# Five scheduling edits in a memory-recurrent attention and gated MLP training kernel: row blocks of the first projections, the queues of lead-in loads, and where two bulk copies stand

## The chip, the cores and the metric

The kernel runs on one core of one Trainium2 chip, as one launch. The metric is the device time of that launch in microseconds (us), taken as the median of several executions. The engines are TensorE (PE, with its weight loads shown apart as PEld), VectorE (DVE), ScalarE (ACT), GpSimd (POOL) and SyncE (SP); SP, ACT and POOL also issue DMA transfers.

## The reference, cut to what matters

The program computes a forward pass and all its gradients. S = 2048 tokens of width D = 640, H = 32 heads of width 128, segments of 32 tokens, M = 8 memory rows, hidden width F = 1728.

```python
xn = layernorm(x)
mem = mem0
for s in range(64):                       # segments, one after the other
    h = concat([mem, xn[:, 32*s:32*s+32]])            # 40 rows
    q, k, v = h @ Wq, h @ Wk, h @ Wv
    p = softmax(where(mask, q @ k.T / sqrt(128), -1e9))
    o = (p @ v) @ Wo
    mem = o[:8]; outs.append(o[8:])
g = silu((silu(xn @ w1) * (xn @ w3)) @ w2)
out = x + concat(outs) * g
# outputs: out, and the gradients of x, mem0, Wq, Wk, Wv, Wo, w1, w3, w2 under grad_out
```

Since each segment's memory rows come from the segment before, the attention part is a chain of 64 steps forward, and of 64 steps backward.

## The kernel before, in words

The kernel is a sequence of stages that share one core. Inside most stages the instructions of each engine keep the order in which they are written (`in_order` ties every instruction to the one before it on its engine), so a wait on one engine holds up all that is written behind it on that engine, and a DMA issue that waits holds up the later issues on its queue.

1. **`phase12_ln_Bfwd`** (0 to 283 us): layer norm and forward MLP. At its end, while the last MLP tiles (`up`) are interleaved, it computes V for the first `NB0` = 672 tokens in full 512-column products, and stores it to the DRAM tensor `QVX`.
2. **`first_part`** (283 to 406 us): the same first 672 rows for K (`KX`) and then Q (`QVX`). Each of these three projections goes through `first_rows` (L356): for a block of 112 rows (6 blocks) and a group `cg` of 1024 columns (4 groups), two PSUM tiles of 112 x 512, each with five accumulating matmuls (640 = 5 x 128), an eviction by DVE or ACT into a staging tile, and a store. During the K projection the stage also loads `Wq` and `Wo` (`fetch`), turns `Wv` head by head on PE and stores it to `WVT` (`turn_w`), and later turns the first K rows (`kload`, `kturn`). The loop index `n` counts row block and column group together, 0 to 47; loads and clears are tied to values of `n`.
3. **`recurrence`** (406 to about 1640 us): 64 forward steps. Each step projects the 32 x 640 activations of its segment in a packed form (`packed_half`): four matmuls of 32 rows each stand side by side in the PE array, at column positions 0, 32, 64 and 96, each with another group of 1024 weight columns.
4. **`phase3b_out`** (to about 1794 us): the rest of the output projection, and the turned weights `WoT`, `WqT`, `WkT` by transposing DMA loads. It also builds the list `later`: 16 DRAM-to-DRAM copies that the backward chain issues one per step on the POOL queue, from step t = 53 on. The first two are the copies of the token rows of the gradient `GS` into `GWO`, which holds token and memory rows in blocks of 120.
5. **`phase4_Abwd`** (1794 to 2995 us): a lead-in of 19 units `pro` (a unit is a tile of three segments and four heads), and then 64 backward steps. A unit is loaded by `ld`, turned on PE with ACT evictions into `gvT` and `gOT` (`turn`), multiplied (`dprob`), put through the softmax gradient on DVE (`dsoft`) and reduced to memory rows (`gmem`). `ld` issues four loads: memory rows `QVM`, token rows `QVS` (both into `gqv`), the gradient `gor`, and the probabilities `PR` (into `gPr`). For the first 19 units three of the four are issued on POOL and the fourth on SP; later units use SP for all. The stores of `gvT` to `VTD` and of `gdS` to `DSR` are issued on POOL, each out of two buffers.
6. **`phase6_Awgrads`** (2995 to 4224 us): gradients of Wv, Wk, Wq and of the attention input. Eight rounds `qd` of 512 columns; a round has 22 positions `p` (one unit each) and then the weight gradient itself, 15 long sums `wg` at L1562. `ld_w` (L1444) loads three weight slices per round: Wv from its stored turned copy `WVT`, Wk and Wq by transposing DMA loads (`turned_load`, L271). `ld` (L1456) loads a unit ahead, five units at most. In the first round `ld_to(3)`, `ld_w(0)` and `ld_to(5)` stand in this order on the SP queue.
7. **`phase6b_gWo`** and **`phase5_Bbwd_ln`** (4224 us to the end): the gradient of Wo, which reads `GWO`, and the backward MLP and layer norm.

Of the kernel before, what the change touches and what calls it, by code (L numbers as in the profile page):

```python
# [9 lines left out]
BF16 = mybir.dt.bfloat16  # L10
F32 = mybir.dt.float32
# [5 lines left out]
P = 128  # L17
# [23 lines left out]
class K:  # L41
# [109 lines left out]
    def setup_dram(self):  # L151
        tc = self.tc
        S, D, T, H, F = self.S, self.D, self.T, self.H, self.F
        HD = self.HD
        dp = self.ctx.enter_context(tc.tile_pool(name="scratch", bufs=1, space=bass.MemoryType.DRAM))
        self.dp = dp
        mk = lambda name, shape, dt=BF16: dp.tile(list(shape), dt, name=name, uniquify=False)
        self.XN = mk("XN", (S, D))
        self.SLT = mk("SLT", (F, S))
        self.DUT = mk("DUT", (F, S))  # L160
        self.HB = mk("HB", (F, S))
        self.DZ = mk("DZ", (S, D))
# [36 lines left out]
        self.GSP = mk("GSP", (8, 3, 160, 512))  # L199
        self.WVT = mk("WVT", (P, H, D))  # L200

    def x_src(self, tl, w, c0, c1):
        return self.tok_src(96 * tl, self.geo(tl)[2], w, c0, c1)
# [65 lines left out]
def turned_load(k, dst, src):  # L269

    k.nc.sync.dma_start_transpose(dst, src)  # L271
# [83 lines left out]
    return pt  # L355


def first_rows(k, ps, stage, xs, off, W, dst, x0, cg, nb=112, tag="b0pb", w=1024, q=None):

    nc = k.nc  # L360
    for b in range(2):
        c0 = cg * 1024 + b * 512
        if w == 512 or b == 0:
            st = stage()
        pb = ps.tile([nb, 512], F32, name="b0pb", tag=tag)
        for dc in range(k.DC):
            nc.tensor.matmul(pb[:], xs[:, dc, x0 - off:x0 - off + nb], W[:, dc, c0:c0 + 512],
                             start=(dc == 0), stop=(dc == k.DC - 1))
        s0 = b * 512 if w == 1024 else 0
        k.copy(st[:, s0:s0 + 512], pb[:], eng='vs'[b])  # L370
        if w == 512 or b == 1:
            (q or nc.sync).dma_start(dst[x0:x0 + nb, cg * 1024 + (b * 512 if w == 512 else 0):cg * 1024 + b * 512 + 512], st[:])


def phase3_Afwd(k, W4, Wv, Wk_):
# [18 lines left out]
def first_part(k, Wv, Wk_, Wq, Wo, kTs, vt, hxs, rest):  # L394
    nc, tc = k.nc, k.tc
    DC, H, HD = k.DC, k.H, k.HD
    with tc.tile_pool(name="b0", bufs=1) as io, tc.tile_pool(name="b0s", bufs=4) as stp, \
# [4 lines left out]
        xs = io.tile([P, DC, k.NB0], BF16, name="b0x")  # L402
# [45 lines left out]
            turn_w()  # L448
        n = 0
        for W, dst in ((Wk_, k.KX[:, :]), (Wq, k.QVX[:, 0])):  # L450
            for x0 in range(0, k.NB0, 112):
                for cg in range(4):
                    if n % 2 == 1 and fetch:
                        nc.scalar.dma_start(*fetch.pop(0))
                    first_rows(k, ps, lambda: stp.tile([112, 1024], BF16, name="b0st", tag="b0st"), xs, 0, W, dst, x0, cg, q=nc.gpsimd)
                    turn_w()
                    if zero:
                        nc.gpsimd.memset(zero.pop(0)[:], 0.0)
                    if n >= 26 and n % 2 == 0 and (n - 26) // 2 < 9:
                        i = (n - 26) // 2  # L460
                        if i > 0:
                            kturn(i - 1)
                        if i < 8:
                            kload(i)
                    if n == 20:
# [4 lines left out]
                    if n == 44:  # L470
# [435 lines left out]
def phase3b_out(k, Wo, W0, W4):  # L906


    nc, tc = k.nc, k.tc
    D, DC, H, HD, T = k.D, k.DC, k.H, k.HD, k.T  # L910
    WT = {}
# [7 lines left out]
    with tc.tile_pool(name="oio", bufs=1) as io, tc.tile_pool(name="oac", bufs=1, space=bass.MemoryType.PSUM) as pa, \  # L919
# [5 lines left out]
        st, acc = {}, {}  # L925
# [90 lines left out]
        while g0:  # L1016
# [2 lines left out]
        in_order(k, start)  # L1019
    WT["v"] = W4.tile([P, H, D], BF16, name="WvT", tag="w3")  # L1020

    n = k.NTL - 1
    later = [(k.GWO[0:120 * n, :].rearrange("(t r) d -> t r d", r=120)[:, 0:96], k.GS[0:96 * n, :].rearrange("(t r) d -> t r d", r=96)),
             (k.GWO[120 * n:120 * n + 32, :], k.GS[96 * n:k.S, :])]

    for s in range(3):
        t0 = (2, 0, 1)[s]
# [14 lines left out]
def phase4_Abwd(k, out2, WoT, WvT, WkT, WqT, later):  # L1042
# [3 lines left out]
    with tc.tile_pool(name="gst", bufs=1) as st, tc.tile_pool(name="gchain", bufs=1) as ch, \  # L1046
# [185 lines left out]
        def ld(tl, qd, eng=None):  # L1232

            ns, nm, nx, n = k.geo(tl)
            c0, h0 = qd * 512, qd * 4
            i = cnt["l"]
            cnt["l"] += 1
            early = i < len(pro)
            g = i % 6 if early else (i - len(pro) + 1) % NG
            if g < NG:  # L1240
                gor = gors[g][:]
                qv = fl.tile([120, 2, 512], BF16, name="gqv", tag="gqv", bufs=4)[:]
                Pr = fl.tile([120, 4, P], BF16, name="gPr", tag="gPr", bufs=4)[:]
            else:
                x = xb[:, g - NG]
                qv = x[:, 0:1024].rearrange("p (i c) -> p i c", i=2)
                gor = x[:, 1024:1536]
                Pr = x[:, 1536:2048].rearrange("p (h c) -> p h c", h=4)
            t0 = 3 * tl
            q = nc.gpsimd if early else nc.sync  # L1250
            q.dma_start(
                qv[nx:n], k.QVM[t0:t0 + ns, :, qd // 2, :, 512 * (qd % 2):512 * (qd % 2) + 512].rearrange("t r i c -> (t r) i c"))
            k.load_x(qv, 0, k.x_src(tl, "qv", c0, c0 + 512), q)
            k.load_x(gor, 0, k.g_src(tl, c0, c0 + 512), nc.sync)
            q.dma_start(Pr[0:n], k.PR[tl][:, h0:h0 + 4, :])
            uu["l", tl, qd] = qv, gor, Pr

        def turn(tl, qd):
# [152 lines left out]
def phase6_Awgrads(k, X, out0, out3, out4, out5):  # L1411
# [12 lines left out]
    with tc.tile_pool(name="h6i", bufs=3) as io, tc.tile_pool(name="h6", bufs=1) as hp, \  # L1424
# [20 lines left out]
        def ld_w(qd):  # L1445
            c0 = qd * 512
            ws = []
            for i, src in enumerate((k.A_Wv, k.A_Wk, k.A_Wq)):
                w = gp.tile([P, 4, D], BF16, name="w6", tag=f"w6{i}")
                if i == 0:  # L1450
                    nc.sync.dma_start(w[:], k.WVT[:, 4 * qd:4 * qd + 4, :])
                else:
                    turned_load(k, w[:], src.rearrange("d h e -> d (h e)")[:, c0:c0 + 512])
                ws.append(w)
            Ws[qd] = ws
# [145 lines left out]
        for qd in range(8):  # L1601
            u0 = NTL * qd
            for p in range(NTL):
# [113 lines left out]
def phase12_ln_Bfwd(k: K, Wv, Wk_):  # L1717
# [6 lines left out]
    with tc.tile_pool(name="bw", bufs=1) as wp, tc.tile_pool(name="bio", bufs=2) as io, \  # L1724
# [165 lines left out]
        turned_load(k, xb[:, :, 0:224], k.XN[448:672, :])  # L1890
        up_ld(NBLK - 1, 0)
        up_ld(NBLK - 1, 1)
        xa, off = xnTs[NBLK], 0
        stg = []

        def stage():
            stg.append(ln.tile([112, 512], BF16, name="b0st", tag=f"xt{len(stg) % 8}"))
            return stg[-1]
        for n, (x0, cg) in enumerate([(x0, cg) for x0 in range(0, k.NB0, 112) for cg in range(4)]):
            if n % 3 == 1 and n // 3 < TB:  # L1900
                up(NBLK - 1, n // 3)
                if n < 6:
                    up_ld(NBLK - 1, n // 3 + 2)
            if x0 == 448:
                xa, off = xb, 448
            first_rows(k, ps, stage, xa, off, Wv, k.QVX[:, 1], x0, cg, tag="pg", w=512)
        in_order(k, start)


# [271 lines left out]
```

## Time and profile before

| | |
|---|---|
| time, median of 3 | 4798.12 us (4796.45 to 4808.65) |
| span of the profiled execution | 4795.1 us |
| PE busy | 4474.0 us (93%) |
| DVE, ACT, POOL busy | 2248.3, 1591.1, 2109.1 us |
| mean granted TensorE clock | 0.974 of full speed |
| DMA moved | 841.31 MB, mean 175 GB/s |

PE busy over the whole span is the mean over stages with different limits, so the table alone doesn't say what any one edit is worth. The windows view gives, for each stretch of time, the busy time of each engine, the granted clock (PEclk, where 1.00 is full speed) and the mean busy share of the 16 DMA engines; the timeline gives instructions in order, with the idle time before each in brackets and what ended it. In both, a queue's DMA issues are listed as SPq, ACTq or POOL.

### The profile page before, as it was taken

Reading aid. Unit: us, or ns where it says so; the run is one execution under the profiler, and the core shown is the slowest. Engines: PE = TensorE matmul, PEld = TensorE weight load, DVE = VectorE, ACT = ScalarE, POOL = GpSimd, SP = SyncE. Lnnn points to the kernel's source line nnn. Section 1 sums busy time; section 2 is a strip of 40 time slices with the busy share of each in tenths; the row PEclk is TensorE's granted clock in tenths of the full one; section 3 lists DMA queues with packets and bytes.
Section 4 is the critical chain, followed back from the end, with each engine's and each line's share of the span. In section 5 each row is a group of like instructions: output and inputs, shape, how many; then the busy total and the mean of one; then the engine's idle time right before and its main releaser. Section 6 shows DMA issues by size and latency. Waiting matters only on the chain. (4 is left out here: it accounts for less than half of the span.)

```text
span 4795.1 us, 160346 instructions
## 1 busy us (share of the span) xinstructions
PE 4474.0 (93%) x64434; PEld 2864.5 (60%) x64704; DVE 2248.3 (47%) x7164; ACT 1591.1 (33%) x4371; POOL 2109.1 (44%) x3541
## 2 busy tenths in 40 slices
PE   8898999999999787989999998899999999999999
PEld 4455555555555464656666665666666666667665
DVE  8634666666666524545555553332234322311460
ACT  5432555555544522323333332322233222300000
POOL 6522555555555405445544443643355433411340
PEclk9999999999999796999999999899999999999999
DMA  8763566666555497777777773943455433669774
GB/s 271 234 231 101 174 178 180 179 181 181 178 166 169 128 218 206 209 210 207 219 210 208 212 211 111 207 131 108 108 151 154 133 109 106 190 193 223 158 179 98
DMA packets 997844, 841.31 MB, mean 175 GB/s; under 512 B 542558, under 2 KB 880402, under 8 KB 995096
## 3 DMA queue, kind: packets, MB, share of 16 engines
q1 hardware_dynamic: 784201, 552.53, 41.9%
q0 software_dynamic: 130592, 229.98, 16.4%
q10 hardware_dynamic: 82307, 48.52, 3.9%
q8 instruction: 511, 8.37, 0.8%
q14 instruction: 233, 1.91, 0.1%
HBM read 473.80 MB, written 311.48 MB: 164 GB/s over the span
## 5 line engine op out<-in xcount | busy, mean ns | idle before, releaser
L1562 PE MATMUL wg<-gr,hr 128*128 128x512 bf16 x2352 | 519.1, 379 | 2.5
L1543 PE MATMUL g<-w,ghacc 128*128 128x320 bf16 x3072 | 459.8, 300 | 0.8
L1562 PEld LDWEIGHTS <-hr 128*128 128x128 bf16 x2400 | 233.9, 98 | 278.8
L1543 PEld LDWEIGHTS <-ghacc 128*128 128x128 bf16 x3072 | 288.4, 98 | 104.2 <-ACT ghacc L92 2.2
L307 PEld LDWEIGHTS <-hx 128*32 128x32 bf16 x7680 | 176.7, 96 | 168.9 <-issue 5.7
L90 DVE CAST wgo<-wg 128x512 bf16<-128x512 f32 x72 | 49.8, 692 | 471.3 <-PE wg L1562 462.9
L90 DVE CAST stg<-bank 128x512 bf16<-128x512 f32 x256 | 177.0, 692 | 161.4 <-PE bank L307 154.9
L778 POOL DMA_DIRECT2D OR<-xv x163 | 90.4, 555 | 354.0 <-ACT xv L92 334.0
L92 ACT COPY ghacc<-t6g 128x768 bf16<-128x768 bf16 (+1 forms) x176 | 137.2, 780 | 304.1 <-PE t6g L1525 303.1
L1508 POOL DMA_DIRECT2D GSP<-grs x48 | 25.7, 547 | 477.6 <-ACT grs L1500 474.8
L326 PEld LDWEIGHTS <-gkv 128*8 128x8 bf16 x8192 | 179.0, 87 | 89.0 <-issue 7.1
L1268 POOL DMA_DIRECT2D VTD<-gvT x176 | 129.4, 741 | 219.7 <-ACT gvT L1267 199.9
L730 POOL TENSOR_TENSOR xP<-xP,xrz 120x480 bf16<-120x480 bf16 x163 | 161.4, 990 | 75.1 <-DVE xrz L729 46.2
L710 ACT ACTIVATE xP<-xsp,xnm 120x120 bf16<-120x120 f32 (+1 forms) x540 | 186.6, 373 | 20.5 <-DVE xnm L692 17.2
L1549 DVE TENSOR_TENSOR ghacc<-ghacc,g 128x320 f32<-128x320 f32 x192 | 93.5, 487 | 210.0 <-PE g L1543 210.0
L92 ACT CAST wgo<-wg 128x512 bf16<-128x512 f32 x48 | 28.1, 586 | 479.8 <-PE wg L1562 421.4
L1297 DVE SCALAR_TENSOR_TENSOR gdS<-gdp,Dx,gPr 120x120 bf16<-120x120 f32 (+1 forms) x680 | 182.8, 331 | 0.0
L326 PE MATMUL bank<-Wo,oTm 128*32 128x320 bf16 x4032 | 158.2, 312 | 18.8 <-DVE oTm L608 18.8
L326 PE MATMUL gbank<-WvT,gkv 128*8 128x320 bf16 x4096 | 171.0, 311 | 4.6 <-issue 3.6
L1315 POOL DMA_DIRECT2D GXP<-gks x157 | 91.1, 581 | 190.9 <-ACT gks L1313 184.3
L326 PE MATMUL gbank<-WkT,gkv 128*8 128x320 bf16 x4096 | 163.9, 301 | 3.9 <-issue 2.1
L307 PE MATMUL bank<-Wq,hx 128*32 128x512 bf16 x2560 | 163.0, 384 | 2.6 <-DVE stg L90 2.6
(354 smaller groups left out, 10920.6 us busy)
## 6 DMA issues: line engine op xcount, KB each, us to landing
QVS<-stg SPq DMA_DIRECT2D x128, 256.0 KB
vTt<-VTD SPq DMA_DIRECT2D x64, 320.0 KB
VTD<-gvT POOLq DMA_DIRECT2D x168, 120.0 KB, 3.8
DSR<-gdS POOLq DMA_DIRECT2D x168, 120.0 KB, 3.2
dS<-DSR SPq DMA_DIRECT2D x168, 120.0 KB
P<-PR SPq DMA_DIRECT2D x168, 120.0 KB
PR<-xP POOLq DMA_DIRECT2D x163, 120.0 KB, 3.3
OR<-xv POOLq DMA_DIRECT2D x163, 120.0 KB, 3.1
```

The source lines that it names most:

```text
L90: return nc.vector.tensor_copy(out, in_)
L92: return nc.scalar.copy(out, in_)
L307: k.nc.tensor.matmul(bank[32 * g:32 * g + 32, :], x[:, dc, :], W[:, dc, c0:c0 + 512], start=(dc == 0), stop=(dc == k.DC - 1), tile_positio ...
L326: k.nc.tensor.matmul(pm[p0:p0 + nq, 0:320], x[:, h, :], W[:, h, 320 * b:320 * b + 320], start=(first and i == 0), stop=(last and i == 15), ...
L710: nc.scalar.activation(Pb[0:n, j, 0:n], sp[0:n, j, :], ACT.Exp, bias=nmx[0:n, j:j + 1], scale=k.scale, accum_out=Z[0:n, j:j + 1])
L730: eng.tensor_tensor(Pb[0:n, :, 0:n], Pb[0:n, :, 0:n], bc_last(rz[0:n], n), ALU.mult)
L1268: nc.gpsimd.dma_start(k.VTD[tl][:, :, h0:h0 + 4, :], vTq[:])
L1297: nc.vector.scalar_tensor_tensor(dS[0:n, j, 0:n], dp[0:n, j, :], Dx[0:n, j:j + 1], Pr[0:n, j, 0:n], op0=ALU.subtract, op1=ALU.mult)
L1315: (nc.sync if (tl, qd) in pro else nc.gpsimd).dma_start(k.GXP[tl, :, qd, 0:ns], ks[:].rearrange("p s i h m -> p s i (h m)"))
L1543: nc.tensor.matmul(pg[:], ring[:, i, j, r0:r0 + P], Ws[qd][i][:, j, 320 * h:320 * h + 320], start=(i == 0 and j == 0), stop=(i == 2 and j ...
L1549: nc.vector.tensor_tensor(a, a, pg[:], ALU.add)
L1562: nc.tensor.matmul(pw[:], hr[:, tl, dc * P:(dc + 1) * P], grs[i][:, tl, :], start=(tl == 0), stop=(tl == NF - 1))
```

## The change

Five edits:

1. The three first projections use blocks of 128 rows: five blocks of 128, and a rest of 32 rows that is computed by the new `last_rows` in the packed form of the recurrence. `n` then runs from 0 to 41, and what was tied to values of `n` is moved. From `n` = 36 on the stores are issued on SP instead of POOL.
2. The V projection at the end of `phase12_ln_Bfwd` puts its two PSUM tiles under two tags (`pg`, `pu`) instead of one.
3. In the lead-in of the backward chain, the loads of `QVS` and `PR` are issued on SP.
4. The slices of `WkT` and `WqT` that the first round of `phase6_Awgrads` needs are stored to a DRAM tensor `WQK` during the backward chain (they take the place of the two `GWO` copies at the head of `later`), and loaded from there with plain DMAs.
5. The copy of the `GS` rows into `GWO` is made in seven pieces and a rest in the rounds of `phase6_Awgrads`, at position p = 18, on POOL.

The purpose is less PE time for the first rows, a shorter queue of loads ahead of the stores in the lead-in, no bulk copy beside the backward chain, and no transposing DMA ahead of the first units' loads.

```diff
-def first_rows(k, ps, stage, xs, off, W, dst, x0, cg, nb=112, tag="b0pb", w=1024, q=None):
+def first_rows(k, ps, stage, xs, off, W, dst, x0, cg, tag="b0pb", w=1024, q=None):
...
-        pb = ps.tile([nb, 512], F32, name="b0pb", tag=tag)
+        pb = ps.tile([P, 512], F32, name="b0pb", tag=tag if isinstance(tag, str) else tag[b])
         for dc in range(k.DC):
-            nc.tensor.matmul(pb[:], xs[:, dc, x0 - off:x0 - off + nb], W[:, dc, c0:c0 + 512],
+            nc.tensor.matmul(pb[:], xs[:, dc, x0 - off:x0 - off + P], W[:, dc, c0:c0 + 512],
...
+def last_rows(k, ps, stage, xs, off, W, dst, tag="b0pb", w=1024, q=None):
+
+    x0 = k.NB0 - 32
+    for b in range(2):
...
+        packed_half(k, pb, xs[:, :, x0 - off:x0 - off + 32], W, b)
+        s0 = b * 512 if w == 1024 else 0
+        k.copy(st[:, s0:s0 + 512], pb[:], eng='vs'[b])
...
@@ first_part
-            for x0 in range(0, k.NB0, 112):
-                for cg in range(4):
+            for x0 in list(range(0, k.NB0 - 32, P)) + [None]:
+                for cg in range(4 if x0 is not None else 1):
...
+                    if x0 is None:
+                        last_rows(k, ps, stage, xs, 0, W, dst, q=nc.gpsimd if n < 36 else nc.sync)
+                    else:
+                        first_rows(k, ps, stage, xs, 0, W, dst, x0, cg, q=nc.gpsimd if n < 36 else nc.sync)
...
-                    if n >= 26 and n % 2 == 0 and (n - 26) // 2 < 9:
-                        i = (n - 26) // 2
+                    if n >= 24 and n % 2 == 0 and (n - 24) // 2 < 9:
+                        i = (n - 24) // 2
...
@@ phase3b_out
-    n = k.NTL - 1
-    later = [(k.GWO[0:120 * n, :].rearrange("(t r) d -> t r d", r=120)[:, 0:96], k.GS[0:96 * n, :].rearrange("(t r) d -> t r d", r=96)),
-             (k.GWO[120 * n:120 * n + 32, :], k.GS[96 * n:k.S, :])]
+    later = [(k.WQK[i], WT[w][:, 0:4, :]) for i, w in enumerate("kq")]
...
@@ phase4_Abwd, ld
             q = nc.gpsimd if early else nc.sync
...
-            k.load_x(qv, 0, k.x_src(tl, "qv", c0, c0 + 512), q)
+            k.load_x(qv, 0, k.x_src(tl, "qv", c0, c0 + 512), nc.sync)
             k.load_x(gor, 0, k.g_src(tl, c0, c0 + 512), nc.sync)
-            q.dma_start(Pr[0:n], k.PR[tl][:, h0:h0 + 4, :])
+            nc.sync.dma_start(Pr[0:n], k.PR[tl][:, h0:h0 + 4, :])
...
@@ phase6_Awgrads, ld_w
-                if i == 0:
-                    nc.sync.dma_start(w[:], k.WVT[:, 4 * qd:4 * qd + 4, :])
+                if i == 0 or qd == 0:
+                    nc.sync.dma_start(w[:], k.WVT[:, 4 * qd:4 * qd + 4, :] if i == 0 else k.WQK[i - 1])
...
@@ phase6_Awgrads, the positions p of a round
+                if p == 18:
+                    if qd < 7:
+                        nc.gpsimd.dma_start(k.GWO[360 * qd:360 * qd + 360, :].rearrange("(t r) d -> t r d", r=120)[:, 0:96],
+                                            k.GS[288 * qd:288 * qd + 288, :].rearrange("(t r) d -> t r d", r=96))
+                    if qd == 6:
+                        nc.gpsimd.dma_start(k.GWO[120 * NTL - 120:120 * NTL - 88, :], k.GS[96 * NTL - 96:S, :])
...
@@ end of phase12_ln_Bfwd
-        for n, (x0, cg) in enumerate([(x0, cg) for x0 in range(0, k.NB0, 112) for cg in range(4)]):
+        for n, (x0, cg) in enumerate([(x0, cg) for x0 in range(0, k.NB0 - 32, P) for cg in range(4)]):
...
-            first_rows(k, ps, stage, xa, off, Wv, k.QVX[:, 1], x0, cg, tag="pg", w=512)
+            first_rows(k, ps, stage, xa, off, Wv, k.QVX[:, 1], x0, cg, tag=("pg", "pu"), w=512)
+        last_rows(k, ps, stage, xb, BLK, Wv, k.QVX[:, 1], tag=("pg", "pu"), w=512)
```

More of the change, by code (lines that the diff above doesn't have):

```diff
@@ L200, in setup_dram @@
         self.WVT = mk("WVT", (P, H, D))
+        self.WQK = mk("WQK", (2, P, 4, D))
     def x_src(self, tl, w, c0, c1):
@@ L371, in first_rows @@
         if w == 512 or b == 1:
-            (q or nc.sync).dma_start(dst[x0:x0 + nb, cg * 1024 + (b * 512 if w == 512 else 0):cg * 1024 + b * 512 + 512], st[:])
+            (q or nc.sync).dma_start(dst[x0:x0 + P, cg * 1024 + (b * 512 if w == 512 else 0):cg * 1024 + b * 512 + 512], st[:])
+def last_rows(k, ps, stage, xs, off, W, dst, tag="b0pb", w=1024, q=None):
+    x0 = k.NB0 - 32
+    for b in range(2):
+        if w == 512 or b == 0:
+            st = stage()
+        pb = ps.tile([P, 512], F32, name="b0pb", tag=tag if isinstance(tag, str) else tag[b])
+        packed_half(k, pb, xs[:, :, x0 - off:x0 - off + 32], W, b)
+        s0 = b * 512 if w == 1024 else 0
+        k.copy(st[:, s0:s0 + 512], pb[:], eng='vs'[b])
+        if w == 512 or b == 1:
+            c0, c1 = (b * 512 if w == 512 else 0), b * 512 + 512
+            (q or k.nc.sync).dma_start(dst[x0:k.NB0].rearrange("r (g c) -> g r c", g=4)[:, :, c0:c1], st[:])
 def phase3_Afwd(k, W4, Wv, Wk_):
@@ L450, in first_part @@
         for W, dst in ((Wk_, k.KX[:, :]), (Wq, k.QVX[:, 0])):
-            for x0 in range(0, k.NB0, 112):
-                for cg in range(4):
+            for x0 in list(range(0, k.NB0 - 32, P)) + [None]:
+                for cg in range(4 if x0 is not None else 1):
                     if n % 2 == 1 and fetch:
                         nc.scalar.dma_start(*fetch.pop(0))
-                    first_rows(k, ps, lambda: stp.tile([112, 1024], BF16, name="b0st", tag="b0st"), xs, 0, W, dst, x0, cg, q=nc.gpsimd)
+                    stage = lambda: stp.tile([P, 1024], BF16, name="b0st", tag="b0st")
+                    if x0 is None:
+                        last_rows(k, ps, stage, xs, 0, W, dst, q=nc.gpsimd if n < 36 else nc.sync)
+                    else:
+                        first_rows(k, ps, stage, xs, 0, W, dst, x0, cg, q=nc.gpsimd if n < 36 else nc.sync)
                     turn_w()
@@ L464, in first_part @@
                             kload(i)
-                    if n == 20:
+                    if n == 18:
                         mem_ld()
@@ L469, in first_part @@
                         nc.gpsimd.memset(kTs[1][:], 0.0)
-                    if n == 44:
+                    if n == 38:
                         for i in range(2):
@@ L1889, in phase12_ln_Bfwd @@
         xb = io.tile([P, DC, BLK], BF16, name="xnT_b", tag="xnT_b")
-        turned_load(k, xb[:, :, 0:224], k.XN[448:672, :])
+        turned_load(k, xb[:, :, 0:160], k.XN[512:672, :])
         up_ld(NBLK - 1, 0)
@@ L1896, in stage @@
         def stage():
-            stg.append(ln.tile([112, 512], BF16, name="b0st", tag=f"xt{len(stg) % 8}"))
+            stg.append(ln.tile([P, 512], BF16, name="b0st", tag=f"xt{len(stg) % 8}"))
             return stg[-1]
-        for n, (x0, cg) in enumerate([(x0, cg) for x0 in range(0, k.NB0, 112) for cg in range(4)]):
+        for n, (x0, cg) in enumerate([(x0, cg) for x0 in range(0, k.NB0 - 32, P) for cg in range(4)]):
             if n % 3 == 1 and n // 3 < TB:
@@ L1903, in phase12_ln_Bfwd @@
                     up_ld(NBLK - 1, n // 3 + 2)
-            if x0 == 448:
-                xa, off = xb, 448
-            first_rows(k, ps, stage, xa, off, Wv, k.QVX[:, 1], x0, cg, tag="pg", w=512)
+            if x0 == BLK:
+                xa, off = xb, BLK
+            first_rows(k, ps, stage, xa, off, Wv, k.QVX[:, 1], x0, cg, tag=("pg", "pu"), w=512)
+        last_rows(k, ps, stage, xb, BLK, Wv, k.QVX[:, 1], tag=("pg", "pu"), w=512)
         in_order(k, start)
```

## The prediction

> **What bounds the kernel now.** I read the windows view first, cut at the stages that the five edits touch, to see which stretches are bound by PE and which wait. Columns: the window, its length, busy us of PE, PEld, DVE, ACT, POOL (with counts), granted PE clock, busy share of the 16 DMA engines, GB/s.
>
> ```profile
> 208.00:283.00 75.00, 69.46 (x357) 42.32 (x356) 29.55 (x49) 20.26 (x34) 13.40 (x20) 1.00 0.48 149
> 289.00:352.00 63.00, 59.40 (x362) 37.37 (x363) 21.77 (x36) 20.78 (x36) 27.63 (x41) 1.00 0.94 331
> 352.00:406.00 54.00, 54.00 (x290) 32.83 (x292) 20.40 (x34) 14.57 (x26) 16.05 (x26) 1.00 0.45 139
> 1794.00:1886.00 92.00, 59.47 (x551) 33.37 (x561) 40.35 (x249) 26.23 (x104) 56.61 (x98) 0.63 0.81 224
> 2082.00:2107.00 25.00, 16.92 (x308) 9.22 (x297) 6.80 (x35) 2.40 (x9) 6.24 (x13) 0.73 0.53 184
> 2996.00:3020.00 24.00, 9.18 (x84) 6.91 (x84) 4.21 (x10) 5.29 (x9) 18.39 (x34) 0.50 1.00 211
> 3107.00:3172.00 65.00, 64.68 (x312) 30.05 (x316) 7.07 (x12) 4.60 (x8) 6.60 (x12) 1.00 0.26 67
> ```
>
> The reader sees three kinds. The V, K and Q projections (first three rows) are PE-bound: 54.00 of 54.00 us in the Q part. The lead-in (1794 to 1886) and the start of the weight-gradient stage (2996 to 3020) have an idle PE at a low clock beside nearly full DMA engines. The window at 2082 lies in the backward chain, with PE at 17 of 25 us, yet the DMA engines half free. The last row, the `wg` sums of a round, has the DMA engines at 0.26.
>
> Then the waits in these stretches. In the lead-in (who waited for what: total, times, longest):
>
> ```profile
> ACT gvT L1266 <- DMA VTD<-gvT: 39.4, 11, 9.1
> DVE gdS L1294 <- DMA DSR<-gdS: 15.5, 6, 5.1
> PE gvpt L1264 <- DMA gor<-GX: 10.0, 1, 10.0
> ```
>
> ACT waits for its two `gvT` buffers, that is for stores that POOL issues behind the loads. Next the timeline. The first two lines are POOL's around step t = 53; the next are SP's and PE's at the start of the weight-gradient stage; the last is one whole packed projection of a backward step.
>
> ```profile
> 2078.62 0.66 POOL L1406 DMA_DIRECT2D GWO<-GS  x1
> 2099.41 0.60 POOL L1315 DMA_DIRECT2D GXP<-gks  x1 [5.73 <-DMA GWO<-GS]
> ...
> 3001.92 5.56 SPq L271 DMA_TRANSPOSE w<-in_A_Wk_dram  x1
> 3007.53 5.91 SPq L271 DMA_TRANSPOSE w<-in_A_Wq_dram  x1
> 3013.48 0.60 SPq L1462 DMA_DIRECT2D dS<-DSR  x1
> ...
> 3016.57 0.58 PE L1483 MATMUL t<-ident,dS 120*128 120x120 bf16 x4 [11.48 <-DMA dS<-DSR]
> ...
> 2975.60 2.34 PE L307 MATMUL gbank<-WoT,gox 128*32 128x512 bf16 x40 [0.29 <-DVE gox L1226]
> ```
>
> PE stood still for 11.48 us at 3016.57 because the load of `dS` was issued only at 3013.48, after two transposing loads that held SP for 5.56 + 5.91 us. The bulk copy issued at 2078.62 has POOL wait for it 20 us later. The chain of waits begins at 2992 and so gives the path in the weight-gradient stage: `dS` loads at its start, then PE.
>
> **What the Trainium skill says.** "TensorE: Matmul & The Clock Gate", section "Part 3: Packing small matmuls", says that matmuls at different tile positions run concurrently. The trace agrees: 40 packed matmuls of 512 columns take 2.34 us, where the unpacked ones of the projections take 0.216 us each (in the timeline 38 of them take 8.37 us, of which 0.38 is the last one's own). "DMA: Bandwidth & Descriptors", section "Issuing engines are not separate DMA queues", says that all issues end on the same 16 engines, and that another issuing engine saves only issue time. This speaks for a small gain of the edit to the lead-in (DMA share 0.81). The trace qualifies it: there the order behind one queue costs ACT 39.4 us of waiting. The first of these pages, in its section "Part 1: The HAM clock gate", says that PE is granted half its clock after an idle window and the full one after about 3.4 us of work; the trace has 0.50 in the 24 us from 2996.
>
> **The change part by part.**
>
> *128-row blocks (edits 1 and 2).* Before: 6 blocks x 4 groups x 2 halves x 5 = 240 matmuls per projection. A matmul streams 512 columns whether it has 112 or 128 rows, so after: 5 x 40 = 200 at 0.216 = 43.2 us, plus one packed rest of 40 matmuls, 2.34 us: 45.5 against 51.8 us, 6.3 us less. Three projections: 18.9 us. The evictions (0.69 us DVE, 0.59 us ACT) fall from 48 to 42 and have slack: DVE is busy 20.4 of 54 us. In the V part PE lost 5.5 us waiting for evictions of two PSUM buffers; four may give back 0.5 us (0 to 3). In the K part the DMA engines are at 0.94, above 1.0 between 300 and 340 us, and blocks of 128 put 14% more bytes of K stores into each group while the same weights are fetched; DVE and ACT already wait 20.4 us for these stores. Yet PE has four PSUM buffers before it notices: I take 1.5 us back (0 to 5). In the Q part the last stores now stand on SP with `kload` behind them: an SP issue that waits for an eviction delays a K load, which `kturn` on PE needs two groups (4.3 us) later; 0.3 us (0 to 2). Sum: 18.9 + 0.5 - 1.5 - 0.3 = 17.6, bounds 12 to 22. The moved clears and loads cost nothing: POOL is busy 16 of 54 us.
>
> *Lead-in loads on SP (edit 3).* POOL issues 5 DMAs per unit at about 0.6 us, 19 units: some 57 us, which is its 56.61 in the window. Three per unit remain, 34 us. The first `VTD` store was issued at 1810.86, behind 18 load issues, though `gvT` was ready at 1804.9; with six loads left ahead it can go at about 1805, so the longest wait (9.1 us) largely falls. SP takes 38 more issues at 0.35 to 0.6 us; behind them stand the WvT loads and the `GXP` stores, none urgent. But SP's `GXP` store waits for `gmem` in order, so loads behind it still keep the pace of compute. The upper bound is the DMA engines: (1 - 0.81) x 92 = 17 us, less the 4 us of the stage's opening in which nothing can be loaded yet, 13. The lower is 0. I take 6.
>
> *No bulk copy at t = 53, two stores instead (edits 4 and 5, first half).* Between neighbouring starts of L1178 in the timeline a step takes 17.02 us; the step with the copy takes 28.23. The packets of that copy are 42 of 61,440 bytes with 2.57 us each, and SP's `Qst` loads and POOL's stores wait meanwhile. Removing it gains 11.2. The two new stores move 0.66 MB each in rows of 5120 bytes; a load with such packets (`w<-WVT`) has 128 packets of 0.27 us, 2.2 us of the 16 engines. The nearest other copies in the list, the two of `SR<-FS`, cost their steps 3.5 and 0.4 us. I take 1.2 for both stores (0 to 4). Net 10, bounds 7 to 11.
>
> *Plain loads in the first round (edit 4, second half).* SP's issue falls from 11.47 to about 0.9 us, so `dS` of the fourth unit could come 10.6 us earlier. But the DMA engines are at 1.00 there, and the two loads still stand ahead of `dS` in SP's queue. The transposing loads have 5120 packets of 256 bytes at 34.5 ns, 11.0 us of 16 engines; the plain ones 256 of 5120 bytes at 0.274 us, 4.4 us. So 6.6 us, bounds 3 and 11.
>
> *Copies in pieces (edit 5, second half).* Each of seven has six packets of 2.57 us, some 1 us of all engines, at most 18 us if they stand in one row. They are issued at p = 18; behind them on POOL are memory rows of units for the next round, which PE needs after the 65 us of `wg`, and no PE instruction of that stretch takes new data. Nothing (0 to 3 in all). The Wo stage reads `GWO` a round later.
>
> Sum: 17.6 + 6 + 10 + 6.6 = 40.2, so 4798.1 - 40.2 = 4757.9.
>
> **The rivals.** (a) *The DMA engines bind wherever they are near 1.* Then the lead-in gains nothing, the K part gives back 5 us, the first round gains 3, and the stores cost their upper 4: 12 + 0 + 7 + 3 = 22, 4776 us. For it: shares of 0.81, 0.94 and 1.00. Against: the half-free DMA engines at 2082 and the fully PE-bound Q part. (b) *Order, not bandwidth, was the limit everywhere.* The upper bounds: 22 + 13 + 11 + 11 = 57, 4741 us. For it: 39.4 us of ACT waits on stores, and 11.48 us behind two issues. Against: the same shares. (c) *Slower.* The SP queue becomes the lead-in's limit, as loads stand behind `GXP` stores for which SP already waits 43.4 us there (+20 us), and each piece costs its round what the whole copy cost a step, 7 x 11.2 = 78: 4798.1 - 18 - 10 - 7 + 20 + 78 = 4861. Against: the DMA share of 0.26 in `wg`, and that loads on SP need buffers freed by the same `gmem`.
>
> **How the numbers follow.** The forecast near 4758 gets 0.62, rival (a) 0.22, rival (b) 0.13, rival (c) 0.03. The range, 4739 to 4778, holds the forecast and the times of (a) and (b) with a margin of 2 us for the measurement. Faster by over 0.3% (under 4783.7) 0.93; within it 0.04, from a case worse than (a); slower 0.03.
>
> **What would show each step.** `b0pb` with 200 matmuls of 128 rows per projection and a packed L307-like group at its end, the Q part near 47.5 us; no step of the backward chain near 28 us; the wait of PE for `dS` near 5 us instead of 11.48; ACT's wait for `VTD` well under 39.4 us; rounds 2 to 7 of the weight-gradient stage unchanged at about 150 us. Wrong would be: PE waiting in the K part for `b0st`, the lead-in still 92 us, or a `wg` stretch longer than 65 us.

## The result, and the profile after

The changed kernel takes 4764.94 us (median of 4, 4760.79 to 4769.97) against 4797.28 us before: the ratio is 0.9933, with a 95% interval of 0.9907 to 0.9959, so some 32 us less (20 to 45). Run once more beside later experiments it gave 0.9919 (0.9897 to 0.9940). The forecast was 40.2 us less, inside both intervals.

The same view as in the prediction, busy time by windows, of the changed kernel, cut at the same stages: V, K and Q part, lead-in, the step that had the bulk copy, the start of the weight-gradient stage, and the `wg` sums of its first round.

```profile
209.00:272.00 63.00, 62.48 (x357) 31.84 (x356) 27.61 (x46) 18.51 (x31) 13.53 (x21) 1.00 0.53 175
281.00:336.00 55.00, 53.47 (x340) 26.65 (x340) 19.25 (x31) 17.66 (x30) 23.95 (x36) 0.96 0.97 344
336.00:389.00 53.00, 50.68 (x314) 24.21 (x314) 18.77 (x32) 14.09 (x24) 14.43 (x20) 0.97 0.55 178
1782.00:1868.00 86.00, 55.61 (x539) 30.80 (x537) 40.30 (x250) 26.64 (x102) 34.62 (x59) 0.64 0.83 236
2057.00:2075.00 18.00, 16.77 (x389) 10.88 (x388) 9.94 (x52) 5.15 (x18) 8.60 (x16) 1.00 0.91 241
2967.00:2991.00 24.00, 13.48 (x130) 10.54 (x131) 6.20 (x14) 6.38 (x11) 19.12 (x36) 0.55 0.86 257
3075.00:3140.00 65.00, 65.00 (x317) 30.01 (x316) 6.80 (x12) 4.60 (x8) 6.63 (x12) 1.00 0.25 66
```

The V part has lost 12 us and PE is now busy all through it. The Q part was full of PE work before (54.00 of 54.00) and now has 2.3 us of idle time. The lead-in is shorter, but its PE is still at a clock of 0.64 beside DMA engines at 0.83: POOL's load fell from 56.61 to 34.62 us as forecast, and the time by only 4. The step at 2057 is an ordinary one. At 2967 PE does more in its 24 us than before (13.48 against 9.18), and still waits.

Lengths of stages, between first or last matmuls of each, from the traces of before, changed, and the experiments (us; e11 is the best version found):

```
                                  before  changed  again   e1      e2      e3      e4      e11
V, first to last product           73.8    61.6    61.6    61.6    73.8    73.8    73.8    61.7
last V to first K product           6.6     9.7    10.0    10.1     6.7     6.7     6.7     8.1
K part                             62.5    55.1    55.0    55.2    64.5    64.3    62.4    54.4
Q part                             53.9    52.4    52.9    50.3    53.9    53.9    53.9    51.0
first forward step                 24.2    26.5    26.4    26.9    22.8    23.1    24.5    20.7
(sum of these five)               220.9   205.2   205.9   204.1   221.7   221.7   221.1   195.9
forward steps 2 to 63            1178.3  1181.2  1183.2  1179.7  1177.6  1180.8  1173.2  1185.5
output projection stage           115.5   114.6   116.6   120.5   118.9   114.4   117.3   115.2
lead-in, with its opening          90.0    86.1    86.9    88.8    84.1    89.5    92.1    84.1
backward steps 1 to 14            254.2   240.9   244.6   254.8   251.4   243.1   262.7   242.5
end of chain to first wg          116.5   113.3   113.5   119.9   120.0   117.6   114.5   118.1
first to last wg stretch         1051.3  1049.1  1050.4  1051.6  1051.6  1050.3  1049.2  1050.1
```

Between the two profiles of before and changed, 36.4 us apart, the five rows at the top give 15.7, the lead-in 3.9, the backward steps 13.4, the first round 3.3, the later rounds 2.1; the forward steps take 2.9 back, and small rows the rest. Rows that no edit touches scatter: the output projection stage from 114.4 to 120.5, the forward steps from 1173.2 to 1185.5. That is why the parts are judged below by the length of their own stage, and the sum by the times. Each length is from one profile, so a difference is trusted only where it is larger than its row's scatter between kernels with the same code in that stage.

### The profile page after: what moved, and what is told of

Read it like the earlier page. It is cut to its first block, busy times and chain, and to the rows that moved or that the text cites. A ratio compares the mean times of both kernels' runs of the same rounds, so it can differ in the third digit from the quotient of the medians.

```text
span 4758.7 us, 160539 instructions
## 1 busy us (share of the span) xinstructions
PE 4485.7 (94%) x64704; PEld 2830.8 (59%) x64704; DVE 2241.9 (47%) x7155; ACT 1587.1 (33%) x4362; POOL 2085.9 (44%) x3499
## 5 line engine op out<-in xcount | busy, mean ns | idle before, releaser
L730 ACT ACTIVATE xP<-xsp,xnm 120x120 bf16<-120x120 f32 (+1 forms) x540 | 186.6, 374 | 20.9 <-DVE xnm L712 17.7
```

What stands on the lines that cost most here:

```text
L730: nc.scalar.activation(Pb[0:n, j, 0:n], sp[0:n, j, :], ACT.Exp, bias=nmx[0:n, j:j + 1], scale=k.scale, accum_out=Z[0:n, j:j + 1])
```

## The experiments

**e1: blocks and tags alone** (edits 1 and 2 on the kernel before).

> The kernel before with edits 1 and 2 alone. If the parts add as read from the two traces: the V part about 62 us instead of 74, K plus Q about 107.5 instead of 116.4, PE waiting about 5.4 us instead of 2.6 in the first forward step, and the lead-in, the backward step with the bulk copy (28 us between starts of L1178's like) and the first round as before; the time 14 to 18 us shorter. Rival, the DMA engines bind the K part: K alone stays within 2 us of 62.5 and the whole gains under 10 us.

Ratio 0.9989 (0.9977 to 1.0001). The five rows fall to 204.1, 16.8 us less, much as in the changed kernel (15.7); K alone falls by 7.3, so the DMA engines don't hold the K part. The whole time shows only 5.3 us less (11 less to 0.5 more), so the expected 14 to 18 us are missed. Its profile is 9.9 us shorter, with 5.1 us more in the output projection stage and 3.4 more in the first round, both without an edit. Each of the two lies in the scatter of its row; whether they belong to the edit isn't settled. What is shown of this part is the gain in its own stages, not that it all reaches the end of the kernel.

**e2: lead-in loads on SP alone.**

```diff
-            k.load_x(qv, 0, k.x_src(tl, "qv", c0, c0 + 512), q)
+            k.load_x(qv, 0, k.x_src(tl, "qv", c0, c0 + 512), nc.sync)
...
-            q.dma_start(Pr[0:n], k.PR[tl][:, h0:h0 + 4, :])
+            nc.sync.dma_start(Pr[0:n], k.PR[tl][:, h0:h0 + 4, :])
```

> The kernel before with edit 3 alone. If order on POOL was the limit: ACT waits under 10 us for VTD stores instead of 39.4, and the lead-in from the last product of the stage before to the first backward step takes 86 us instead of 90, so 3 to 6 us less in all, with the wait now on the GXP stores on SP (about 18 us). If bandwidth is the limit: the ACT wait moves entirely to other transfers and the lead-in stays at 89 to 91 us. If SP becomes the limit: over 92 us.

Ratio 0.9996 (0.9982 to 1.0010), not told from no change by the time. The lead-in takes 84.1 us, 5.9 less than before. Its waits in the list of who waited for whom:

```profile
ACT gks L1313 <- DMA GXP<-gks: 16.6, 6, 5.2
ACT gvT L1266 <- DMA VTD<-gvT: 7.3, 3, 4.8
```

and in the changed kernel:

```profile
ACT gks L1331 <- DMA GXP<-gks: 18.3, 6, 5.6
ACT gvT L1284 <- DMA VTD<-gvT: 8.0, 4, 4.5
```

ACT's wait for `VTD` falls from 39.4 to 7.3 and 8.0 us, and a wait of 17 to 18 us for the `GXP` stores, which the list of before doesn't have, takes part of its place: these stores are issued on SP, where they now stand behind three loads of a unit instead of one.

**e3: the copy in pieces alone** (edit 5; nothing in its place in the list, so that the twelve copies `HRO<-FS` behind it move two steps forward).

```diff
-    later = [(k.GWO[0:120 * n, :].rearrange("(t r) d -> t r d", r=120)[:, 0:96], k.GS[0:96 * n, :].rearrange("(t r) d -> t r d", r=96)),
-             (k.GWO[120 * n:120 * n + 32, :], k.GS[96 * n:k.S, :])]
+    later = []
...
+                if p == 18:
+                    if qd < 7:
+                        nc.gpsimd.dma_start(k.GWO[360 * qd:360 * qd + 360, :].rearrange("(t r) d -> t r d", r=120)[:, 0:96],
...
```

> The kernel before with edit 5 alone: the GWO copy in pieces, nothing in its place in the list, so that the later copies stand two steps earlier. If the bulk copy is what cost its step and the one after: no step over 22 us, the 64 backward steps 12 to 14 us shorter, rounds 2 to 8 of the weight-gradient stage unchanged at 150 us each. Rival: the pieces cost each round what the copy cost a step; rounds longer by 1 us or more each and the gain under 6 us.

Ratio 0.9972 (0.9955 to 0.9988), 13.4 us: the one part whose gain the times show alone. The first 14 backward steps take 243.1 us against 254.2, and the rounds are unchanged (1050.3 against 1051.3). In the trace of the changed kernel the 42 packets of 61,440 bytes come in seven groups of six, each over within 7 us of its issue (from 3068.2 to 3075.0 in the first round, where `wg` begins at 3074.7), two waves of three packets of 2.3 to 3.3 us.

**e4: plain loads in the first round alone** (edit 4; the bulk copy stays).

```diff
+    later += [(k.WQK[i], WT[w][:, 0:4, :]) for i, w in enumerate("kq")]
...
-                if i == 0:
-                    nc.sync.dma_start(w[:], k.WVT[:, 4 * qd:4 * qd + 4, :])
+                if i == 0 or qd == 0:
+                    nc.sync.dma_start(w[:], k.WVT[:, 4 * qd:4 * qd + 4, :] if i == 0 else k.WQK[i - 1])
```

> The kernel before with edit 4 alone (the bulk copy stays, the two WQK stores follow at the end of the list). If the loads of the fourth unit stand behind 2 MB of weights in SP's queue: PE waits 8 to 10 us for dS instead of 11.5, the first round 3 to 4 us shorter, the whole gain 2 to 4 us. If issue time was the limit: the wait falls to 1 to 2 us and the first round gains 9 to 11 us.

Ratio 0.9995 (0.9983 to 1.0007). PE's longest wait for `dS` is 8.5 us, the first round 114.5. The five kernels with transposing loads (before, e1, e2, e3, e5) have 116.5 to 120.0, mean 118.1; the eight with plain ones in this order have 113.3 to 114.5, but for one of 118.1 (e11), mean 114.4. So some 4 us, and the issue time of 10 us was not what it was worth. Why e11 has 118.1 isn't known.

**e5: the two PSUM tags alone** (blocks of 112 rows).

```diff
-        pb = ps.tile([nb, 512], F32, name="b0pb", tag=tag)
+        pb = ps.tile([nb, 512], F32, name="b0pb", tag=tag if isinstance(tag, str) else tag[b])
...
-            first_rows(k, ps, stage, xa, off, Wv, k.QVX[:, 1], x0, cg, tag="pg", w=512)
+            first_rows(k, ps, stage, xa, off, Wv, k.QVX[:, 1], x0, cg, tag=("pg", "pu"), w=512)
```

> The kernel before with the two PSUM tags alone (edit 2, blocks of 112 rows). If the V part's extra gain comes from PSUM buffers: PE waits there fall from 5.6 us (for ACT and DVE evictions) to under 1.5, and the V part from first to last product takes 68 to 69 us instead of 73.8, though part may be lost again before the K part. If two buffers were enough, as the prediction took it: 73 us.

The V part takes 68.0 us, 5.8 less, and the gap before K stays at 6.6. PE's waits for evictions in the V part of the kernel before (total, times, longest):

```profile
PE b0pb L367 <- ACT b0st L92: 2.9, 4, 0.7
PE b0pb L367 <- DVE sl L1793: 1.4, 1, 1.4
PE b0pb L367 <- DVE b0st L90: 1.3, 4, 0.3
```

The list of e5 for the same part has none of the three: the tags were worth what PE had waited, 5.6 us, all of it. (Ratio 0.9988, 0.9973 to 1.0003.)

**e6: the packed rest ahead of the last block, the K loads one `n` later** (on the changed kernel).

```diff
-            for x0 in list(range(0, k.NB0 - 32, P)) + [None]:
+            for x0 in [0, P, 2 * P, 3 * P, None, 4 * P]:
...
-                    if n >= 24 and n % 2 == 0 and (n - 24) // 2 < 9:
-                        i = (n - 24) // 2
+                    if n >= 25 and n % 2 == 1 and (n - 25) // 2 < 9:
+                        i = (n - 25) // 2
...
+            if (x0, cg) == (BLK, 1):
+                last_rows(k, ps, stage, xb, BLK, Wv, k.QVX[:, 1], tag=("pg", "pu"), w=512)
             first_rows(k, ps, stage, xa, off, Wv, k.QVX[:, 1], x0, cg, tag=("pg", "pu"), w=512)
-        last_rows(k, ps, stage, xb, BLK, Wv, k.QVX[:, 1], tag=("pg", "pu"), w=512)
```

> The changed kernel with the packed rest of 32 rows ahead of the last block of 128 in all three projections, and the K loads and turns one value of n later (from 25). If the slow store of the rest at the end of the Q part holds up the first forward step: PE waits under 3 us there instead of 5.4, that step takes 24 us instead of 26.5, and the turn of the first K rows no longer waits 2.3 us, so Q 48 to 50 us instead of 52.4; the gap before K 6.6 instead of 9.7. In all 7 to 10 us less than the changed kernel from V to the second forward step. Rival, the wait is the SP queue's own and not the rest's: the first step stays at 26 us.

It was made for a wait that the prediction hadn't. In the timeline of the changed kernel, at the end of the Q part and the start of the forward chain, the rest's store on SP and the eviction and product behind it:

```profile
389.63 0.56 SPq L388 DMA_DIRECT2D QVX<-b0st  x1
395.78 1.29 DVE L90 CAST stg<-bank 128x512 bf16<-128x512 f32 x2 [7.14 <-DMA QVX<-b0st]
396.52 2.32 PE L308 MATMUL bank<-Wq,hx 128*32 128x512 bf16 x20 [5.44 <-DVE stg L90]
```

The first step's staging tile lies where the rest's did, so DVE waits until that store has landed, and PE 5.44 us. The same wait in the kernel before:

```profile
410.58 2.33 PE L307 MATMUL bank<-Wq,hx 128*32 128x512 bf16 x20 [2.58 <-DVE stg L90]
```

With the rest in the middle the first step takes 20.1 us instead of 26.5 and the gap before K 7.4 instead of 9.7, both of the kind expected of the store. But Q takes 55.1 us, where 48 to 50 were expected: the K load that stands behind the rest's store on SP, issued at 376.94, now comes late (e6, the turn of the seventh group of K rows).

```profile
383.61 0.34 PE L459 MATMUL kpt<-ident,kr 96*128 96x96 bf16 x4 [3.45 <-DMA kr<-KX]
```

The sum of the five rows is 199.9 against 205.2; ratio 0.9926 (0.9898 to 0.9953).

**e7: the GXP stores of the lead-in on POOL** (on the changed kernel).

```diff
-            (nc.sync if (tl, qd) in pro else nc.gpsimd).dma_start(k.GXP[tl, :, qd, 0:ns], ks[:].rearrange("p s i h m -> p s i (h m)"))
+            nc.gpsimd.dma_start(k.GXP[tl, :, qd, 0:ns], ks[:].rearrange("p s i h m -> p s i (h m)"))
```

> The changed kernel with the GXP stores of the lead-in on POOL, which has three DMAs per unit left. If the GXP stores behind the loads on SP are the new wait: the ACT wait for them (18.3 us) goes under 5 us and the lead-in (last product before it to the first backward step, 86.1 us) is 3 to 8 us shorter. If the DMA engines limit (share 0.88 from the seventh unit on): 84 to 87 us, with the wait gone elsewhere. If POOL's order is the limit again: over 88.

The lead-in takes 88.2 us, no shorter than the 86.1 and 86.9 of the changed kernel. The wait for `GXP` is still 13.8 us and that for `VTD` is up at 14.8:

```profile
ACT gvT L1284 <- DMA VTD<-gvT: 14.8, 7, 9.2
ACT gks L1331 <- DMA GXP<-gks: 13.8, 8, 5.3
```

So the second wait can't be moved away as the first was: what one queue is relieved of, the other pays for. The run doesn't tell order from bandwidth. Its 88.2 us fall under the expectation's "POOL's order is the limit again", but e6, whose lead-in is that of the changed kernel, has 88.4; and the DMA share in the last 70 us of e7's lead-in is 0.90. (Ratio 0.9946, 0.9924 to 0.9969.)

**e8: two more units' loads ahead of the weights** (on the changed kernel).

```diff
-        ld_w(0)
-        ld_to(5)
+        ld_to(5)
+        ld_w(0)
```

> The changed kernel with the loads of the fourth and fifth unit issued ahead of the three weight slices of the first round. If dS of the fourth unit stands behind 2 MB in SP's queue: PE's wait for it falls from 8.7 us to 1 to 3, a later wait for the weights of 1 to 3 us takes part of it back, and the first round is 3 to 6 us shorter than 113. If the 16 engines are simply full: the wait moves to the weights whole and the round stays at 112 to 114 us.

The rival's outcome came: the wait moved whole. The first round takes 115.7 us, no shorter than the 113.3 and 113.5 of the changed kernel. PE's waits in it, in the changed kernel:

```profile
PE t L1501 <- DMA dS<-DSR: 15.9, 5, 8.7
PE r6p L1511 <- DMA r<-QVS: 1.8, 1, 1.8
```

and in e8:

```profile
PE t L1501 <- DMA dS<-DSR: 7.8, 3, 6.3
PE g L1561 <- DMA w<-WVT: 6.0, 1, 6.0
PE r6p L1511 <- DMA r<-QVS: 3.0, 1, 3.0
PE g L1561 <- DMA w<-WQK: 2.8, 2, 2.2
```

PE waits 8.1 us less for `dS` and 8.8 more for the weights. The DMA engines are not simply full, though: their share in the first 24 us is 0.83 (0.86 in the changed kernel). (Ratio 0.9938, 0.9916 to 0.9959.)

**e10: the rest's store in four** (on the changed kernel; the rest stays at the end).

```diff
-            (q or k.nc.sync).dma_start(dst[x0:k.NB0].rearrange("r (g c) -> g r c", g=4)[:, :, c0:c1], st[:])
+            for g in range(4):
+                (q or k.nc.sync).dma_start(dst[x0:k.NB0, 1024 * g + c0:1024 * g + c1], st[32 * g:32 * g + 32, :])
```

> The changed kernel with the store of each packed rest issued as four stores of 32 rows, one for each 1024 columns, at the same place. If it is the access pattern of the one store (128 packets spread over 4.3 us, where a plain block has its 128 in 0.75 us) that holds up the first forward step: the four land within 3 us, PE waits under 3 us there instead of 5.4, and the gap between the V and the K part shrinks from 9.7 to about 7. If it is the place at the end alone, or SP's queue: 5 us and 9.7 us as before.

In the changed kernel the rest's store has its 128 packets of 2048 bytes between 390.8 and 395.1 us, 4.3 us, though little else moves; a plain block's 128 packets of the same size, on the same queue, take some 0.8 us (379.0 to 379.8). A packet takes 0.126 us in the mean instead of 0.088; above all, fewer of them are under way at a time, 3.75 in the mean (128 x 0.126 / 4.3) instead of 13.7. In four stores, the timeline of e10 shows:

```profile
386.86 1.73 SPq L389 DMA_DIRECT2D QVX<-b0st  x4
390.20 1.29 DVE L90 CAST stg<-bank 128x512 bf16<-128x512 f32 x2 [4.33 <-DMA QVX<-b0st]
390.94 2.11 PE L308 MATMUL bank<-Wq,hx 128*32 128x512 bf16 x20 [2.63 <-DVE stg L90]
```

PE's wait is back at 2.63 us, the value before the change, and the first step takes 24.5 us; so the one store with the regrouped rows is the cause there; in four stores the 128 packets take 1.8 us, 8.4 of them at a time. The gap before K stays at 10.1: for it the pattern isn't the cause, and in e6 the place of the rest was. (Ratio 0.9919, 0.9892 to 0.9945.)

**e9 and e11: better versions.** Both have the rest in the middle and the K loads from `n` = 25; e9 has all stores of the K and Q parts on POOL (`q=nc.gpsimd`), e11 keeps the queues and stores the rest in four.

> The kernel with the rest ahead of the last block, K loads from n = 25, and all stores of the K and Q parts on POOL. If K loads behind the slow store on SP cost the Q part its 3.5 us wait in the run with the rest in the middle: no PE wait for them over 1 us, Q 50 to 51.5 us, first forward step about 20 to 24 us, V to second forward step 195 to 198 us (205.2 in the changed kernel, 199.9 in that run). If the wait comes from full DMA engines: 199 to 202.

> The kernel with the rest ahead of the last block, K loads from n = 25, stores as in the changed kernel, but the rest's store in four. If the pattern is the cause: as the run with all stores on POOL, V to second forward step 195 to 198 us. If the order on SP is: 199 to 201.

The five rows sum to 197.8 (e9) and 195.9 us (e11), against 205.2 and 205.9. Both lie in the 195 to 198 us that were expected if the slow store is what delayed the K load in e6: it helps to take the store off that queue (e9), and it helps to make it fast (e11). PE's waits for K loads are 1.0 and 1.6 us. The ratios are 0.9920 (0.9894 to 0.9946) and 0.9904 (0.9880 to 0.9928). e11 is the fastest measured, with a median of 4760.34 us where the changed kernel beside it has 4767.74; the intervals overlap, so its gain of 9 to 10 us in these stages is shown, and its lead in the whole time is only likely.

**e12: the changed kernel once more.**

> The changed kernel once more, as the anchor for the runs beside it and for how far unchanged stages scatter: V to second forward step within 1 us of 205.2; the stage of the output projection and the 63 later forward steps may differ by 3 to 5 us without any edit; the ratio to the kernel before 0.991 to 0.996.

The five rows are 205.9, and the ratio 0.9919 (0.9897 to 0.9940). Its profile is 12 us longer than the first one of the same kernel, spread over stages of which none was edited: this much scatter any single profile has.

## Why the prediction was right, point by point

**128-row blocks (forecast 17.6, measured 15.0 to 16.8 by the lengths of the stages).** The 6.3 us per projection are right: in e5 and e1 the V part goes from 68.0 to 61.6, 6.4 us, and K shortened by 7.4, of which 0.9 is three head turns of `turn_w` that moved to Q with the smaller `n` (0.29 us each). That the sum came out close is luck in part, as its errors cancel: the tags gave 5.3 us more than forecast and K's 1.5 us were not lost; against that stand the gap before K with 3.1 us, Q with 3.6 and the first forward step with 2.3.

*The tags* were given 0.5 with bounds of 0 to 3 and gave 5.8 (e5). The step that failed is that a wait of PE would largely remain with four buffers; every wait, of up to 1.4 us, was for a buffer, and all went.

*The gap before K* grew by 3.1 us (6.6 to 9.7), and the prediction had no term for it. PE waits there for `b0x`, the activations of K and Q; SP's loads of it and K's first product, before and then in the changed kernel:

```profile
285.99 6.49 SPq L271 DMA_TRANSPOSE b0x<-XN  x5
289.26 2.34 PE L367 MATMUL b0pb<-Wk,b0x 128*112 128x512 bf16 x10 [2.20 <-DMA b0x<-XN]
276.94 7.80 SPq L272 DMA_TRANSPOSE b0x<-XN  x6
281.27 3.15 PE L368 MATMUL b0pb<-Wk,b0x 128*128 128x512 bf16 x7 [4.77 <-DMA b0x<-XN]
```

Two things add up. The first load is issued 5.3 us after the start of the last V product instead of 3.3, as SP waits longer for the last V stores to land (3.2 us in all instead of 1.4); with the rest in the middle (e6, e9, e11) it is 3.1 to 3.2, so this half belongs to the rest's place. And from that issue to K's first product 4.3 us pass instead of 3.3. This half is in all nine kernels with blocks of 128 rows (4.3 to 4.9) and in none of the five with 112 (3.3 to 3.4): in the kernel the loads of `b0x` still come in pieces of 112 rows, so a first block of 128 needs two of them. Loads in pieces of 128 were not tried.

*The loss in Q* was given 0.3, with the cause right (the turn of K rows waits for a late load). Q was to be near 47.5 us; with the three head turns it would have been 48.5 (53.9 - 6.3 + 0.9), and it takes 52.4. The loss varies without any edit to this stage: the five kernels with the changed kernel's code there (changed, again, e1, e7, e8) take 50.3 to 54.2. One line of PE's timeline of the changed kernel, at the first such turn:

```profile
353.19 0.34 PE L459 MATMUL kpt<-ident,kr 96*128 96x96 bf16 x4 [2.32 <-DMA kr<-KX]
```

The load was issued at 349.7, behind the last stores of turned heads; besides the 2.32 us the next 20 products took 6.17 us, at a granted clock of 0.72, where later ones take 4.48 at 1.00. Not every such wait has this second cost: in e8 one of 3.34 us is followed by 4.48. With K loads from `n` = 25 and no slow store in their way (e9, e11) the waits are 1.0 and 1.6 us in all; but e1 and e10, whose K loads stand where they stood, have 1.2 and 1.0, so it isn't shown that the later loads cure it.

*The K part* did not give back 1.5: DVE and ACT wait 21.0 us for `KX` stores (20.4 before) and PE still doesn't notice.

**What the prediction missed: the rest's store.** It named the packed products as cheap, 2.34 us, which they are, and gave their store no term. It takes 4.3 us instead of some 0.8 and stands where the next stage waits: 26.4 to 27.1 us for the first forward step in the five kernels with the rest at the end in one store, 22.8 to 24.5 in the five without the block edit.

**Lead-in (forecast 6, measured about 4).** Mean of five profiles without the edit: 90.0 us; of the eight with it (e7 left out): 85.7. Right: POOL's time, the earlier `VTD` stores (the first 13.9 us after the last product of the stage before, instead of 16.9), the end of ACT's long wait; DVE's wait for the `DSR` stores, 15.5 us before, goes as well (0.2). Wrong: that nothing behind the loads on SP is urgent. `GXP` stores release the two `gks` buffers, and ACT waits 18.3 us for them, in the order of its other evictions. What limits the rest is not shown. Bandwidth fits it (the DMA engines are at 0.83, and at 0.88 from 1800 us on), but moving the `GXP` stores to POOL (e7) gains nothing and brings the wait for `VTD` back to 14.8 us, so order on POOL fits as well. "DMA: Bandwidth & Descriptors", section "Issuing engines are not separate DMA queues" in the Trainium skill says that another issuing engine only saves issue time; the 4 of 90 us that it saved here agree in size.

**The bulk copy (forecast 10, measured about 12).** Backward steps 11 to 14, where copy and stores stand: 78.5 to 86.0 us in the five profiles with the copy (79.3 before), mean 81.7; 68.2 to 71.0 in the nine without (68.5 in the changed kernel), mean 69.4. The copy's price was read from one profile, 11.2; it varies, and two of the five have 5 us more. The two `WQK` stores, put at 1.2, hardly show: their two steps in the changed kernel take 17.4 and 17.0 us between starts where the usual one takes 17.0, and e3, which has copies `HRO<-FS` in these places, has 68.6. The prediction took their price from `SR<-FS` as the nearest other copies; the twelve `HRO<-FS` stand nearer, and in the profile before the steps behind ten of them take 16.6 to 17.2 us, behind the other two 17.7 and 18.7.

**Plain loads (forecast 6.6, measured some 4).** The wait for `dS` fell to 8.74 us and not to about 5. The term was worked out from the DMA time that the plain loads save, 6.6 us of 16 engines; but with the engines at 0.86 to 0.87 in this stretch, down from 1.00, not all of it became time: some 3.3 us of the 24 are now idle time of the engines (an estimate, 0.14 x 24). e8 shows that the order of these loads among themselves is not the limit there.

**Copies in pieces (forecast 0, measured 0).** Rounds and `wg` stretches are the same to 0.3 us per round, and the pieces are over about when their `wg` begins.

The sum was 40.2 and is 32 (20 to 45) by the first times and 39 (29 to 49) by the later ones. Rival (a), 22 us, lies inside the first interval and outside the later one, and its grounds hold only for the first round: K gave nothing back, the lead-in gained 4 us, and the copy was worth more. Rival (b), that order was everywhere the limit, put the sum at 57 us, which lies outside both intervals; in the first round e8 speaks against it too. Rival (c) asked for longer rounds and a longer lead-in; neither came. The four parts tried alone add to 23 us by their ratios, with intervals of 12 to 16 us each, so the times can't tell whether the parts help each other.

## What to carry to other kernels

Before a queue is relieved, look at what shares the queue that takes over, and which buffers its stores release: the wait for a store moves with the order, and in this lead-in, with the DMA engines at 0.83, it largely changed its name. Waits for one of two PSUM buffers were worth their whole length once two more were free. When a block changes its size, look at the pieces in which its input is loaded. And the last transfer of a stage counts with its own landing time: put an odd-shaped store in the middle of the stage, ahead of plain ones, or make it several plain ones, and keep it away from where the next stage takes over its memory.

## What the runs showed of the hardware that was not expected

A store of 128 staged rows of 2048 bytes to DRAM took 4.3 us from first to last packet when its rows went to four groups of columns in one DMA, some 0.8 us when they went to 128 rows of the same columns; issued as four DMAs its packets took 1.8 us, and the wait behind it fell from 5.44 to 2.63 us. A DRAM-to-DRAM copy of 42 packets of 61,440 bytes kept some of the 16 engines busy for 18 us (2080.4 to 2098.3) at 2.57 us a packet, some 6 packets at a time (42 x 2.57 / 18), while the DMA share stood near 0.5 and the four steps around it lost 10 to 18 us in the five profiles that have it (four usual steps take 68.4). How many packets are under way at a time differs by DMA: in the mean 3.75 in the store whose target is viewed with an outermost count of 4, 2.9 in the pieces of the copy with an outermost count of 3, 6.0 in the whole copy with 21, and 13.7 in a plain block of 128 rows. This goes with the outermost count of the access pattern; that the count sets it was tried by no run on its own.
